# Attention plus GELU layer: softmax reciprocals on GpSimd as a power, with another table that deals score tiles to engines

## Chip, cores and metric

One Trainium2 chip, one core of it. The metric is the device time of one execution in microseconds (us). The kernel before the change takes 746.38 us (median of 3 runs, 745.35 to 746.84).

## Reference

A layer norm of `x` (2048 rows of 512) feeds two branches, and the result is `x` plus both: attention with 32 query heads of 16 columns that share one key and one value head, and a two-layer network of width 1792 with a tanh GELU.

```python
xn = layernorm(x)                                  # (x - mean) / sqrt(var + 1e-5)
q = (xn @ wq) as 32 heads of 16;  k = xn @ wk;  v = xn @ wv
p = softmax(q k^T * 16**-0.5)                      # 2048 x 2048 for each head
a = concat(p v) @ wo
h = gelu(xn @ w1 + b1) @ w2 + b2
out = x + a + h
```

## The kernel before

**Tiling.** The 2048 queries are four blocks of 512. In each block the 32 heads are eight groups of four, so there are 32 passes over a group. In one pass, 16 key tiles of 128 times four heads give 64 score tiles of 128 keys by 512 queries; 2048 such tiles in all. Three consecutive tiles are a unit (683 units), which takes three banks of PSUM; two sets of three banks alternate. TensorE writes the scores of unit u+2 into the banks that unit u has left (`scores`, line 1042).

**Two engines take the exponential.** ScalarE does most tiles with its Exp (`exp`, line 1065), one instruction for the unit's ScalarE tiles, written to buffer `E`. The other tiles go to VectorE: `p1` (line 1096) reads the scores from PSUM and writes 16-bit whole numbers whose bits are a bf16 approximation of the exponential, into buffer `Dt`. `close_batch` then makes three shifted copies of a batch of such tiles (line 1143: one instruction for one copy, one for two copies at once), and subtracts in place once more (line 1139, one tile each, mostly on GpSimd). Each of the five versions is multiplied with a scaled copy of V and summed by TensorE into the bank `pO` (`pv_mm`, line 1109), so that a VectorE tile costs five matmuls and a ScalarE tile one.

**The table.** `DTAB` has one letter for each unit and says which of its three tiles go to VectorE: `.` none, `0` or `o` the first, `2` or `t` the last, `a` or `A` the first two, `b` or `B` the last two, `x` or `X` all. The letters `o t A B X` also end a batch; a batch ends at six tiles at the latest, and at the end of a pass.

**GELU.** After units 182 and 512 ScalarE leaves the exponentials (`GU`) and does four GELU instructions with a table load before and after; around these units the table has `x` and `X`, so that VectorE goes on alone.

**Normalisation.** Column 16 of each head's block of `pO` is the softmax denominator. When a pass ends, `o_evac` copies `pO` to `Of` (line 1155), and DMAs on SyncE's queue take the denominators to `den` (spread over 128 partitions, 16 numbers in each for a pass) and the numerators to `OfP`. After every second pass a reciprocal over `den` (line 1167, both passes together: 128 by 32) runs on VectorE. A DMA takes it to a small DRAM array, eight DMAs bring it back as rows in `rbP`, and GpSimd multiplies `OfP` by `rbP` (line 1186) into `oTp`, which the output projection reads much later. `den`, `OfP` and `rbP` have two buffers that alternate by pairs of passes. The very last pass has its own code (`o_norm_last`, line 1200), which the change leaves alone.

**The order of the work** comes from a planner in the program: every operation is entered with an assumed duration (`occ`), a latency (`lat`) and a due time; `schedule` plays this through once, and each engine then runs its list in that fixed order, with semaphores. GpSimd operations of kind `"pl"` (lines 1139 and 1186) are placed behind the start of a VectorE instruction that is not marked `lock`; VectorE instructions marked `lock` (lines 1143, 1224 and others, SBUF to SBUF in a fast mode) are placed when the plan has GpSimd done. A `"pl"` operation that finds no such place is given to VectorE. Operations entered with `add("pool", ...)` or `setup` without this kind are placed on GpSimd when they are ready, with no regard to VectorE. `PRO_DUE` is a list with one due time for each of the first 338 operations, by position; the last nine of them are the late set-up (`wol`, `selL`, four `wol` DMAs, `wop`, `b2row` and its DMA), and the position after them is the first score operation.

Of the kernel before, what the change touches and what calls it, by code (L numbers as in the profile page):

```python
# [7 lines left out]
ALU = mybir.AluOpType  # L8
AX = mybir.AxisListType

P = 128
# [26 lines left out]
PL_LAT = 0.06  # L38
# [20 lines left out]
DMASK = {".": (), "0": (0,), "2": (2,), "a": (0, 1), "b": (1, 2), "x": (0, 1, 2),  # L59
         "o": (0,), "t": (2,), "A": (0, 1), "B": (1, 2), "X": (0, 1, 2)}  # L60
CLOSE = "otABX"
DTAB = "000to.2t0000t...t0t0..ooo0.o202t2.t..22t2.2t00.t2.0ot2.22o0002..0.o0o.2t22o2o0.00o.o.t.0o2tt.2.2t2o.2o2.20t0.00t22t.222o.2.2o.02.t2o0o.20ooot2.t0o0.t.o0.0t22t.ot.02oo2.2o.t022t0.2000oxXXXot...ooo2tt.202o0t0.t22t.0t2t.22t2ot.2.0oot2o.000.t0ot.20t.to0t02t0o.ot20oo0.20t2o0o..0o.o20o202.0t2t.2.t00oo..2oo020tt.020.t0o0.2.to.222t20o..t000t.2o.ttt22.2too.t.02ot20.t2.o0t0t2o.o0.t002020o..tt220o0.o2o.2t.22tt.o0.02t0oto0.00t.to2t.2.2tt0002t00o.t00.2t22..2o.00otot..2tt2t.t202..o.00t0.o.02o0.ot0t.2t00.tt2t220.0o00o22.2txXxtottot2o.t00t.2tt.ot22oo.tt.ot0.ooot002.to2o.t22o02.oo0o.2oo2t.220oo000.oo02.t.002o002o20.2t22o2t..2o.tttt0tt.2o.00t0t.0o0200t.t22tt00.2tt0.0o20t.0ttot0.2.ot2t..0o.0.."
YF = 664
Y_ALLOW = 2.0
H_ALLOW = 1.0
# [50 lines left out]
class Prog:  # L116
# [19 lines left out]
    def add(self, eng, fn, r=(), w=(), acc=None, dma=None, occ=0.1, lat=0.15, allow=1.0, kind=None, tag=None, after=(), due=None, lock=False, docc=0.0):  # L136
        if len(self.ops) < len(PRO_DUE):
            due = PRO_DUE[len(self.ops)]
        op = _Op()
        op.lock, op.docc = lock, docc  # L140
        op.eng, op.fn = eng, fn
        op.stream = dma or eng
        op.amt = 16 if dma else 1
        op.need = bool(dma)
        op.ticket = None
        op.occ, op.lat, op.allow, op.kind, op.tag = occ, lat, allow, kind, tag
        op.idx = len(self.ops)
        op.done = False
        op.due = due
        op.rel = None  # L150
        op.pm = any(k == ("bank", 7) or k[0] == ("bank", 7) for k in w)
        deps, sdeps = {}, {}

        def dep(o, raw):
            if o is None or o is op:
                return
            if o.stream == eng == "pe":
                sdeps.setdefault(id(o), (o, False))
                return
            deps[id(o)] = o  # L160
            sdeps[id(o)] = (o, True)

        for k in r:
            dep(self.writer.get(k), True)
            for o in self.accs.get(k, ()):
                dep(o, True)
        for k in w:
            dep(self.writer.get(k), False)
            for o in self.readers.get(k, ()):
                dep(o, False)  # L170
            for o in self.accs.get(k, ()):
                dep(o, False)
        if acc is not None:
            dep(self.writer.get(acc), False)
            for o in self.readers.get(acc, ()):
                dep(o, False)
        op.deps = list(deps.values())
        for o in op.deps:
            o.need = True
        for k in w:  # L180
            self.writer[k] = op
            self.readers[k] = []
            self.accs[k] = []
        for k in r:
            self.readers.setdefault(k, []).append(op)
        if acc is not None:
            self.accs.setdefault(acc, []).append(op)
        for o in after:
            sdeps.setdefault(id(o), (o, True))
        if self.in_chain:  # L190
            o = self.chain.get(eng)
            if o is not None:
                sdeps.setdefault(id(o), (o, False))
            self.chain[eng] = op
        op.sdeps = list(sdeps.values())
        self.ops.append(op)
        return op
# [380 lines left out]
def bass_parallel_sum__grouped_kv_mqa__dense_activation_gelu__prompt_kernel(  # L578
# [30 lines left out]
    bf, f32 = dt.bfloat16, dt.float32  # L609
    i16, i32 = dt.int16, dt.int32  # L610

    with ExitStack() as es:
        def sb(shape, dtype, name):
            return es.enter_context(nc.sbuf_tensor(name, shape, dtype))
# [19 lines left out]
        b1T = sb([P, FT], f32, "b1T")  # L634
        ident = sb([P, P], bf, "ident")
        zeros = sb([P, P], bf, "zeros")
        ones = sb([P, P], bf, "ones")
        mask4 = sb([P, 4], bf, "mask4")
        krow = sb([P, 1], i32, "krow")
# [34 lines left out]
        den = sb([P, 2, 2, 16], f32, "den")  # L674
# [14 lines left out]
        add = pr.add  # L689
# [6 lines left out]
        def dve(fn, r=(), w=(), n=TBW, mode=1, allow=1.0, **kw):  # L696
            return add("dve", fn, r, w, occ=vcost(n, mode), lat=dlat[0], allow=allow, **kw)
# [36 lines left out]
        for a, b, t in X_D:  # L734
            nd += 1
            if a is None:
                o, src, w = ((wvk[:, :, Dh:2 * Dh], A_wk, ["wk_s"]), (wvk[:, :, 0:Dh], A_wv, ["wv_s"]))[b]
                src = src.rearrange("(k p) n -> p k n", p=P)
            else:
                o, src, w = x_sb[:, a:b, :], (x_view[:, a // 2, :, :] if b - a == 2 else x_view[:, a // 2, a % 2:a % 2 + 1, :]), [("x", ti) for ti in range(a, b)]  # L740
# [6 lines left out]
        def setup(fn, r=(), w=(), occ=0.16, due=0.0, lat=0.1, **kw):  # L747
            return add("pool", fn, r, w, occ=occ, lat=lat, due=due, **kw)
# [19 lines left out]
              w=[(k, g, j) for k in ("QT", "QTm") for g in range(NGR) for j in range(HG)])  # L768
        setup(lambda e: e.tensor_copy(wkp[:, :, :, 0:Dh], wvk[:, :, Dh:2 * Dh].unsqueeze(2).to_broadcast([P, DT, 4, Dh])),
              r=["wk_s", "wkp"], w=["wkp"], occ=0.35, due=2.0)  # L770
# [8 lines left out]
              r=["mrow"], w=["isc"], due=10.0)  # L779
# [10 lines left out]
        for gl in range(2):  # L790
            setup(lambda e, gl=gl: e.tensor_copy(sel_diag[gl], mask8[:, 4 * gl:4 * gl + 4].unsqueeze(1).to_broadcast([P, NGR // 2, HG])),
                  r=["mask8", "sel8"], w=["sel8"], due=12.0)
# [3 lines left out]
                    n=1500, due=0.01)  # L796
# [177 lines left out]
        for ft, bk in H_PRO:  # L974
# [4 lines left out]
            due=0.0)  # L979
# [3 lines left out]
            r=["khm", "kcm"], w=[B(3), "kb", "krow"], n=40, due=0.0)  # L983
# [5 lines left out]
        for va, vb_ in ((0, NVA), (NVA, NT)):  # L989
# [3 lines left out]
               w=[vbank(va, vb_)[1], ("Vf", va)], due=DU["vf"])  # L993
            r = ["V1", ("Vf", va)]
            ad(lambda e, va=va, vb_=vb_: e.activation(V1[:, 0, va:vb_, 0:Dh], Vf[:, va:vb_, :], ACT.Copy),
               lambda e, va=va, vb_=vb_: e.tensor_copy(V1[:, 0, va:vb_, 0:Dh], Vf[:, va:vb_, :]), (vb_ - va) * Dh, (vb_ - va) * Dh,
               w=[("V", 0, va)], ra=r, rd=r, mode=2, due=DU["vf"] + 0.1)
# [7 lines left out]
                setup(f, occ=0.93, due=20.0, **rw)  # L1005

        late = [pr.writer["krow"]]
        setup(lambda e: e.memset(wol[:], 0.0), w=["wol"], occ=0.4, due=24.0, after=late)
        setup(lambda e: e.tensor_copy(selL[:], ident[:, 16:113:32]), r=["ident"], w=["selL"], due=24.0, after=late)
        dma("sp", wop[:], A_wo.rearrange("(g p) n -> p g n", p=P), "d_wo", w=["wop"], after=late)  # L1010
# [142 lines left out]
        def o_evac(gg):  # L1153
            i = gg % 2
            dve(lambda e: e.tensor_copy(Of[:, i, :], pO), w=["O", ("Of", i)], allow=0.0)  # L1155
            row = Of[16:17, i, :]
            pp, h = divmod(gg, 2)
            s, sl = pp % 2, pp % NPR
            end = gg == NTB * NGR - 2
            dma("sp", den[:, s, h, :], bass.AP(row.tensor, row.offset, [[32 * row.ap[0][0], HG], [1, TBW]]),  # L1160
                f"d_den{i}", r=[("Of", i)], w=[("den", s, h)])
            for j in range(HG):
                r0 = 64 * h + Dh * j
                dma("sp", OfP[r0:r0 + Dh, s, :], Of[32 * j:32 * j + Dh, i, :], f"d_of{s}{h}", r=[("Of", i)], w=[("OfP", s, h, j)])
            if h or end:
                hs = range(h + 1)
                dve(lambda e: e.reciprocal(den[:, s, 0:h + 1, :], den[:, s, 0:h + 1, :]), r=[("den", s, hh) for hh in hs],
                    w=[("den", s, hh) for hh in hs], n=120 + 16 * h)
                dma("sp", rd_dram[gg - h:gg + 1, :].rearrange("g (p c) -> p g c", p=P), den[:, s, 0:h + 1, :], f"d_rd{s}",
                    r=[("den", s, hh) for hh in hs], w=[("rd", s)])  # L1170
                for hh in hs:
                    for j in range(HG):
                        r0 = 64 * hh + Dh * j
                        src = rd_dram[gg - h + hh:gg - h + hh + 1, j * TBW:(j + 1) * TBW]
                        dma("sp", rbP[r0:r0 + Dh, s, :], bass.AP(src.tensor, src.offset, [[0, Dh], [1, TBW]]), f"d_rb{s}",
                            r=[("rd", s)], w=[("rbP", s, hh, j)])
            if end:
                dve(lambda e: e.memset(oTp[64:P, sl, :], 0.0), r=[("Of", i)], w=[("oTp", sl)], n=200, lock=True)
            if h or end:
                n = 64 if end else P  # L1180
                keys = [(k, s, hh, j) for k in ("OfP", "rbP") for hh in range(h + 1) for j in range(HG)]
                first = pre.pop(sl, [])
                for q in range(2):
                    c = slice(q * TBW // 2, (q + 1) * TBW // 2)
                    onorm[gg - h] = onorm[gg] = add(
                        "pool", lambda e, c=c: e.tensor_tensor(oTp[0:n, sl, c], OfP[0:n, s, c], rbP[0:n, s, c], ALU.mult),  # L1186
                        keys, [("oTp", sl, q)] + first, occ=ON_OCC, lat=PL_LAT, allow=PL_DUE, kind="pl", lock=True,
                        docc=vcost(TBW // 2))
# [166 lines left out]
        first, n = None, 0  # L1355
# [101 lines left out]
```

## Time and profile before

| what | value |
|---|---|
| median of 3 runs | 746.38 us |
| the profiled execution | 746.57 us |
| its span, first to last instruction | 744.8 us |
| what lies around the span in that execution | 1.77 us |
| score tiles to ScalarE / to VectorE (from the table) | 1493 / 555 |

The busy time of an engine is the union of its instructions' records; consecutive records of ScalarE and of VectorE overlap, so that a busy share of 100% doesn't mean that the engine could take no more. Rows of the view by line give the line, the engine, the operation, output and inputs, count, busy time, the mean of one in ns, and the idle time before. Windows are stretches of the span with each engine's busy time.

### The profile page before, as it was taken

Reading aid. Unit: us, or ns where it says so; the run is one execution under the profiler, and the core shown is the slowest. Engines: PE = TensorE matmul, PEld = TensorE weight load, DVE = VectorE, ACT = ScalarE, POOL = GpSimd, SP = SyncE. Lnnn points to the kernel's source line nnn. Section 1 sums busy time; section 2 is a strip of 40 time slices with the busy share of each in tenths; the row PEclk is TensorE's granted clock in tenths of the full one; section 3 lists DMA queues with packets and bytes.
Section 4 is the critical chain, followed back from the end, with each engine's and each line's share of the span. In section 5 each row is a group of like instructions: output and inputs, shape, how many; then the busy total and the mean of one; then the engine's idle time right before and its main releaser. Section 6 shows DMA issues by size and latency. Waiting matters only on the chain.

```text
span 744.8 us, 22099 instructions
## 1 busy us (share of the span) xinstructions
PE 730.0 (98%) x9040; PEld 215.0 (29%) x9042; DVE 731.1 (98%) x1412; ACT 729.7 (98%) x741; POOL 383.1 (51%) x548
## 2 busy tenths in 40 slices
PE   7999999999999999999999999999998999999998
PEld 4322222222232222222222222222232222222223
DVE  7999999999999999999999999999999999999996
ACT  8899999999999999999999999999999999999995
POOL 7434555545533546545656455343543646546560
PEclk9999999999999999999999999999999999999999
DMA  9200100000011010100101110100100101010011
GB/s 310 66 19 17 30 11 19 22 11 16 16 46 30 13 35 18 24 16 16 32 7 26 26 38 18 37 16 15 24 12 24 31 17 38 16 46 17 10 31 37
DMA packets 31198, 23.34 MB, mean 31 GB/s; under 512 B 16385, under 2 KB 25722, under 8 KB 31098
## 3 DMA queue, kind: packets, MB, share of 16 engines
q1 hardware_dynamic: 31098, 21.94, 11.2%
q8 instruction: 72, 1.18, 0.7%
q14 instruction: 28, 0.23, 0.1%
HBM read 13.08 MB, written 2.35 MB: 21 GB/s over the span
## 4 chain that ended last, share of the span: by engine, by line
ACT 62%; PE 22%; DVE 13%; DMA 1%; SPq 1%; issue 1%
ACT E L1065 62%; PE pAll L1109 10%; PE pAll L1042 6%; DVE Dt L1096 6%; PE pAll L714 5%; DVE Dt L1143 5%; DMA b1row<-in_B_b_dram 1%; SPq L721 1%; DVE Of L1155 1%; PE pAll L708 0%; PE pAll L1418 0%; DVE Dt L1139 0%; DVE x_sb L1251 0%; DVE xnT L864 0%; DVE qp L1223 0%
## 5 line engine op out<-in xcount | busy, mean ns | idle before, releaser
L1065 ACT ACTIVATE E<-pAll 128x1024 bf16<-128x1024 f32 (+1 forms) x676 | 680.5, 1285 | 1.6 <-PE pAll L1042 1.5
L1139 POOL TENSOR_SCALAR Dt<-Dt 128x512 int16<-128x512 int16 x454 | 342.3, 754 | 325.9 <-DVE Dt L1143 116.0
L1109 PE MATMUL pAll<-Dt,V 128*32 128x512 bf16 x2775 | 409.4, 386 | 2.6 <-DVE Of L1155 2.3
L1096 DVE TENSOR_SCALAR Dt<-pAll 128x512 int16<-128x512 f32 (+1 forms) x541 | 367.6, 693 | 1.9 <-PE pAll L1042 1.0
L1109 PE MATMUL pAll<-E,V 128*32 128x512 bf16 x1493 | 303.9, 384 | 0.2 <-DVE Of L1155 0.2
L1143 DVE TENSOR_SCALAR Dt<-Dt 128x1024 int16<-128x1024 int16 (+6 forms) x540 | 288.0, 559 | 0.4
L1042 PE MATMUL pAll<-QT,KT 32*128 32x512 bf16 x2048 | 267.4, 385 | 4.5 <-ACT E L1065 2.4
L1042 PEld LDWEIGHTS pAll<-QT,KT 32*128 32x128 bf16 x2048 | 66.8, 91 | 295.3 <-ACT E L1065 283.8
L1109 PEld LDWEIGHTS pAll<-Dt,V 128*32 128x32 bf16 x2775 | 103.3, 95 | 102.5 <-issue 69.6
L1109 PEld LDWEIGHTS pAll<-E,V 128*32 128x32 bf16 x1493 | 72.9, 95 | 44.0 <-issue 33.0
L714 PE MATMUL pAll<-xnT,w_sb 128*32 128x512 bf16 x896 | 84.9, 384 | 0.0
L714 PE MATMUL pAll<-w_sb,x_sb 128*32 128x512 bf16 x448 | 76.4, 384 | 0.0
L714 PE MATMUL pAll<-w_sb,ub 128*32 128x512 bf16 x448 | 64.3, 383 | 0.1
L714 PE MATMUL pAll<-wop,oTp 128*32 128x512 bf16 x256 | 51.9, 383 | 0.0
L1186 POOL TENSOR_TENSOR oTp<-OfP,rbP 128x256 bf16<-128x256 f32 (+1 forms) x28 | 22.5, 809 | 14.6 <-DVE Dt L1143 7.9
L714 PEld LDWEIGHTS pAll<-xnT,w_sb 128*32 128x32 bf16 x896 | 21.4, 95 | 26.6 <-issue 16.8
L714 PE MATMUL pAll<-xnT,wq_sb 128*32 128x512 bf16 x256 | 26.8, 383 | 0.0
L1139 DVE TENSOR_SCALAR Dt<-Dt 128x512 int16<-128x512 int16 x101 | 26.2, 279 | 0.0
L1155 DVE COPY Of<-pAll 128x512 f32<-128x512 f32 x31 | 21.1, 680 | 0.1
L714 PEld LDWEIGHTS pAll<-w_sb,x_sb 128*32 128x32 bf16 x448 | 18.3, 95 | 8.2 <-issue 6.7
L1251 DVE TENSOR_SCALAR ub<-pAll,b1T 128x512 bf16<-128x512 f32 x28 | 20.7, 738 | 0.0
L1251 DVE TENSOR_SCALAR x_sb<-pAll,b1T 128x512 bf16<-128x512 f32 x28 | 20.7, 738 | 0.0
(125 smaller groups left out, 264.5 us busy)
## 6 DMA issues: line engine op xcount, KB each, us to landing
OfP<-Of SPq DMA_DIRECT2D x124, 32.0 KB, 2.0
rbP<-rden_rows SPq DMA_DIRECT2D x124, 32.0 KB, 1.8
w_sb<-in_B_w_dram SPq DMA_DIRECT2D x2, 1792.0 KB, 11.4
x_sb<-in_A_x_dram SPq DMA_DIRECT2D x18, 128.0 KB, 2.3
QT<-qp SPq DMA_DIRECT2D x124, 16.0 KB, 1.8
x_sb<-in_A_x_dram SPq DMA_DIRECT2D x7, 256.0 KB, 3.9
out_dram<-x_sb SPq DMA_DIRECT2D x12, 128.0 KB, 1.9
wq_sb<-in_A_wq_dram SPq DMA_DIRECT2D x1, 512.0 KB, 5.9
```

Of the source, the lines that this page charges most:

```text
L714: add("pe", lambda e, c=c, j=j: e.matmul(o[c, :], l[:, c], rh, start=start, stop=stop, tile_position=(0, 32 * j)), r, [(k, j) for k in w] ...
L721: return add(eng, lambda e: e.dma_start(o, i), r, w, dma=stream, occ=occ, lat=lat, allow=allow, **kw)
L1042: ins = e.matmul(o, l, rh, start=True, stop=True, tile_position=(q0, 0))
L1065: o = act(lambda e: e.activation(E[:, s0:s0 + na, :], bank(b0, na).rearrange("p (a n) -> p a n", a=na), ACT.Exp, scale=LN2 / 128.0), w=[B( ...
L1096: op = dve(lambda e: e.tensor_scalar(Dt[:, s:s + n, :], bank(bk, n).rearrange("p (a n) -> p a n", a=n), float(127 * 128) + SPL_D, SPL_MIN, ...
L1109: add("pe", lambda e, a, b: e.matmul(pO[32 * j:32 * j + 32, :], V1[:, v, kt, :], rhs, start=a, stop=b, tile_position=(0, 32 * j)), r=r + [ ...
L1139: add("pool", lambda e, d=d, k=k: e.tensor_scalar(d, d, 1.0, float(k), ALU.mult, ALU.add), [], [(("D", base[o > 0] + q), o)], occ=PL_OCC, ...
L1143: dve(lambda e, d=view(o, nb), q=view(i, nb), k=k: e.tensor_scalar(d, q, float(k), None, ALU.add), r=keys(i), w=keys(o), n=nb * n * TBW, m ...
L1155: dve(lambda e: e.tensor_copy(Of[:, i, :], pO), w=["O", ("Of", i)], allow=0.0)
L1186: "pool", lambda e, c=c: e.tensor_tensor(oTp[0:n, sl, c], OfP[0:n, s, c], rbP[0:n, s, c], ALU.mult),
L1251: dve(lambda e: e.tensor_scalar(ubs[tb % 2][:, ft, :], pM, b1T[:, ft:ft + 1], None, ALU.add), r=["b1T"], w=M4 + [ukey(tb, ft)], n=TBW + 57 ...
```

## The change

The reciprocals at line 1167 become an element-wise power on GpSimd: `den` to the power of a constant tile `neg1` that holds -1.0, in f32. The tile is filled once in the late set-up, ahead of `wol`. The operation is entered without the kind `"pl"`, with an assumed duration of 0.6 us. The reciprocals of the last pass stay on VectorE. The table `DTAB` is another one, of the same length.

```diff
-DTAB = "000to.2t0000t...t0t0..ooo0.o202t2.t. ... 2000oxXXXot... ... 22.2txXxtottot ... 2ot2t..0o.0.."
+DTAB = "0202o0.0t20to...0t02..022o..022o2t.t. ... o2oo.xXX.Xtt22 ... 000.2Xx2xoA..oo ... 20tot..00..."
...
+        neg1 = sb([P, 2, 16], f32, "neg1")
...
         late = [pr.writer["krow"]]
+        setup(lambda e: e.memset(neg1[:], -1.0), w=["neg1"], due=24.0, after=late)
         setup(lambda e: e.memset(wol[:], 0.0), w=["wol"], occ=0.4, due=24.0, after=late)
...
-                dve(lambda e: e.reciprocal(den[:, s, 0:h + 1, :], den[:, s, 0:h + 1, :]), r=[("den", s, hh) for hh in hs],
-                    w=[("den", s, hh) for hh in hs], n=120 + 16 * h)
+                add("pool", lambda e: e.tensor_tensor(den[:, s, 0:h + 1, :], den[:, s, 0:h + 1, :], neg1[:, 0:h + 1, :], ALU.pow),
+                    ["neg1"] + [("den", s, hh) for hh in hs], [("den", s, hh) for hh in hs], occ=0.6, lat=PL_LAT, allow=0.0)
```

Of the two tables, the parts shown in the middle are units 178 to 190 and 508 to 521, around the two GELU stretches. What the two tables say, counted by the rules above:

| | before | after |
|---|---|---|
| tiles to VectorE | 555 | 555 |
| Exp instructions of 3, 2, 1 tiles | 141, 535, 0 | 143, 531, 2 |
| `p1` instructions | 541 | 539 |
| batches | 270 | 253 |

More of the change, by code (lines that the diff above doesn't have):

```diff
@@ L61 @@
 CLOSE = "otABX"
-DTAB = "000to.2t0000t...t0t0..ooo0.o202t2.t..22t2.2t00.t2.0ot2.22o0002..0.o0o.2t22o2o0.00o.o.t.0o2tt.2.2t2o.2o2.20t0.00t22t.222o.2.2o.02.t2o0o.20ooot2.t0o0.t.o0.0t22t.ot.02oo2.2o.t022t0.2000oxXXXot...ooo2tt.202o0t0.t22t.0t2t.22t2ot.2.0oot2o.000.t0ot.20t.to0t02t0o.ot20oo0.20t2o0o..0o.o20o202.0t2t.2.t00oo..2oo020tt.020.t0o0.2.to.222t20o..t000t.2o.ttt22.2too.t.02ot20.t2.o0t0t2o.o0.t002020o..tt220o0.o2o.2t.22tt.o0.02t0oto0.00t.to2t.2.2tt0002t00o.t00.2t22..2o.00otot..2tt2t.t202..o.00t0.o.02o0.ot0t.2t00.tt2t220.0o00o22.2txXxtottot2o.t00t.2tt.ot22oo.tt.ot0.ooot002.to2o.t22o02.oo0o.2oo2t.220oo000.oo02.t.002o002o20.2t22o2t..2o.tttt0tt.2o.00t0t.0o0200t.t22tt00.2tt0.0o20t.0ttot0.2.ot2t..0o.0.."
+DTAB = "0202o0.0t20to...0t02..022o..022o2t.t.22to.20.o0t.ot0t.020t.20.0.o2002t0t..t2t02o0.0o.t.2t.o200o00.t2.t2.22t2.t2o220.o222o2.t2o..0t02t..0oo22t2t2.22t..t0t00to.t.ot2t2000.o.20.0t.oo2oo.xXX.Xtt22t2222o.t.0o0tt0t.tt.o2t2t020.000..2oo202t.t.o0t0.t00.t.otoo20o02t.2o.t2t0oot022t0.00.2tt00o..0o0t22o0.02.0.2t002.0.o2t202ot.o.o0.20ooo..0tt2ttt.2ot22.0to.0000.o0t.o00t2t20.2o00o.02.tto.0t.0t02000o2o.00.o.2o20o202..222o2o2.o2o2.2o2.t.2t022o202ot..2o0.o2to.020.o022t2..22o000t..to..002o..002o22.ot.22.0o22o.202t00o2.20000.2Xx2xoA..ooot2o20t2.ott22t.00t0t.22oo02.o002.tt.toB0..o0o0o20t..t00.ot2o2o200o0.2oto.2t.2tot.00oo0.2ot000.2t020t22o0..t2t00o00t..0o00tt02tt2.0ot0.o..2o.o0.t02o20tot..00..."
 YF = 664
```

## Prediction

> **What bounds the kernel now.** The page comes first: the span, the busy times and the shares of the chain of waits.
>
> ```profile
> span 744.8 us, 22099 instructions
> PE 730.0 (98%) x9040; PEld 215.0 (29%) x9042; DVE 731.1 (98%) x1412; ACT 729.7 (98%) x741; POOL 383.1 (51%) x548
> ACT 62%; PE 22%; DVE 13%; DMA 1%; SPq 1%; issue 1%
> ```
>
> Three engines stand at 98%, so a busy share names no bound. The chain runs 62% of its time through ScalarE and 13% through VectorE. Windows show where ScalarE has time left (after the stretch and its length: busy time of PE, its weight loads, VectorE, ScalarE, GpSimd; clock, DMA share, GB/s).
>
> ```profile
> 100.00:200.00 100.00, 99.27 (x1232) 28.09 (x1224) 99.68 (x184) 100.00 (x100) 54.44 (x75) 1.00 0.07 16
> 200.00:300.00 100.00, 99.59 (x1246) 29.43 (x1242) 99.57 (x189) 99.62 (x93) 47.70 (x64) 1.00 0.10 26
> 300.00:400.00 100.00, 99.34 (x1213) 28.53 (x1212) 99.92 (x187) 100.00 (x101) 55.05 (x71) 1.00 0.09 20
> ...
> 500.00:600.00 100.00, 96.96 (x1205) 28.78 (x1202) 99.39 (x188) 98.90 (x91) 50.10 (x71) 0.98 0.10 23
> 600.00:700.00 100.00, 98.96 (x1271) 27.37 (x1267) 99.77 (x197) 100.00 (x103) 54.70 (x70) 1.00 0.09 22
> ...
> 734.00:744.80 10.80, 8.04 (x112) 3.69 (x110) 4.42 (x12) 2.86 (x4) 0.00 (x0) 1.00 0.15 49
> ```
>
> ScalarE is idle for 0.38 us in one of these and 1.10 us in another, the two with the GELU stretches, and never in the rest: 1.48 us in all. The last 10.8 us are a tail in which no engine is full. The view of waits says who holds whom.
>
> ```profile
> PEld pAll L1042 <- ACT E L1065: 283.8, 656, 0.8
> ...
> PEld pAll L1042 <- DVE Dt L1096: 8.0, 18, 0.7
> PEld pAll L1109 <- DVE Of L1155: 5.1, 7, 2.8
> PEld pAll L1109 <- POOL Dt L1139: 4.3, 18, 0.4
> ...
> ACT E L1065 <- PE pAll L1042: 1.5, 3, 1.0
> ```
>
> The score matmuls wait for ScalarE's Exp 656 times and for VectorE's first step (L1096) 18 times. Outside the GELU stretches the loop is Exp, scores into the freed banks, Exp; VectorE's share of a unit is nearly always done by then. A faster VectorE is therefore worth something only where it ends a wait.
>
> **The reciprocals leave VectorE.**
>
> ```profile
> L1167 DVE RECIPROCAL den<-den 128x32 f32<-128x32 f32 x15 | 5.1, 340 | 0.0
> L1167 DVE RECIPROCAL den<-den 128x16 f32<-128x16 f32 x1 | 0.2, 243 | 0.0
> ...
> L1143 DVE TENSOR_SCALAR Dt<-Dt 128x1024 int16<-128x1024 int16 x189 | 76.3, 415 | 0.1
> L1143 DVE TENSOR_SCALAR Dt<-Dt 128x512 int16<-128x512 int16 x110 | 29.5, 280 | 0.0
> ```
>
> Removed: 15 x 0.340 + 0.243 = 5.3 us of records. The records overlap, so the time between starts is what VectorE really gets back:
>
> ```profile
> 207.66 0.68 DVE L1096 TENSOR_SCALAR Dt<-pAll 128x512 int16<-128x512 f32 x1
> 208.26 0.34 DVE L1167 RECIPROCAL den<-den 128x32 f32<-128x32 f32 x1
> 208.52 0.65 DVE L1096 TENSOR_SCALAR Dt<-pAll 128x512 int16<-128x512 f32 x1
> ```
>
> The next instruction starts 0.26 us after the reciprocal: 15 x 0.26 + 0.16 (0.24 less the same 0.08) = 4.1 us.
>
> **The table.** ScalarE keeps 1493 tiles in 676 Exp instructions (before 141 + 535, after 143 + 531 + 2).
>
> ```profile
> L1065 ACT ACTIVATE E<-pAll 128x1024 bf16<-128x1024 f32 x535 | 527.0, 1197 | 1.2 <-PE pAll L1042 1.2
> L1065 ACT ACTIVATE E<-pAll 128x1536 bf16<-128x1536 f32 x141 | 224.0, 1619 | 0.3 <-PE pAll L1042 0.3
> ```
>
> If an Exp costs a fixed part and a part for each tile, as these rows allow (0.42 us more for the third tile), equal tiles in equal instructions cost the same: 0. The one-tile form has no row; for its two instructions I take nothing and bound it by 0.1 us each. TensorE keeps its matmuls: 555 x 5 + 1493. VectorE loses 17 batches, 34 instructions of L1143: their elements stay, and by the two L1143 rows the fixed part is 0.280 - (0.415 - 0.280) = 0.145 us, about 0.07 us less between starts by the overlap above: 34 x 0.07 = 2.4 us, 4.9 us at most by the records. Two fewer instructions of L1096 are 0.2 us. VectorE's relief is thus 4.1 + 2.4 + 0.2 = 6.7 us between starts, about 0.9% of its 731.1 us.
>
> What that buys: at least 0, since ScalarE is full; at most the chain's VectorE share in proportion, 13% of 744.8 = 97 us times 0.9% = 0.9 us. I take 0.6, nearer to the top, because the chain's long VectorE pieces are real and the rest is cover by ScalarE.
>
> **The two GELU stretches.** These rows show ScalarE coming back from its GELU work, and the scores it waits for.
>
> ```profile
> 224.25 0.10 PEld L1042 LDWEIGHTS pAll<-QT,KT 32*128 32x128 bf16 x3 [0.42 <-DVE Dt L1096]
> 226.53 0.39 PE L1042 MATMUL pAll<-QT,KT 32*128 32x512 bf16 x3
> 226.97 2.79 ACT L1065 ACTIVATE E<-pAll 128x1536 bf16<-128x1536 f32 x2 [0.32 <-PE pAll L1042]
> 228.70 0.39 PE L1042 MATMUL pAll<-QT,KT 32*128 32x512 bf16 x3
> ...
> 568.18 1.94 ACT L1065 ACTIVATE E<-pAll 128x1024 bf16<-128x1024 f32 x2
> 571.11 4.85 ACT L1065 ACTIVATE E<-pAll 128x1024 bf16<-128x1024 f32 x5 [0.99 <-PE pAll L1042]
> ```
>
> Before, units 183 to 186 and 513 to 515 are all VectorE's; ScalarE returns at 187 and 516 and then idles 0.32 and 0.99 us: 1.31. After, the runs are 183 to 185 and 513 to 514, with 186 (three ScalarE tiles) and 515 (two) ahead of one more all-VectorE unit each. VectorE has three tiles fewer to do before ScalarE's return, so both old holes should go: -1.3. But behind 186 ScalarE's next work is 188, whose scores need the banks of 186: its Exp (1.62) must end, then a start of the matmuls (226.97 + 1.62 = 228.59 to 228.70, so 0.11), the scores (0.39) and the step to the Exp (226.53 + 0.39 to 226.97, so 0.05). That leaves 0.11 + 0.39 + 0.05 = 0.55 us idle, and as much behind 515: +1.1. Together -0.2 us. Bounds: -1.3 if the plan finds cover, +2 if VectorE is also late there.
>
> **What GpSimd gets.** Sixteen powers. The trace has no power; the nearest rows on GpSimd:
>
> ```profile
> L1139 POOL TENSOR_SCALAR Dt<-Dt 128x512 int16<-128x512 int16 x454 | 342.3, 754 | 325.9 <-DVE Dt L1143 116.0 <-PE pAll L1109 73.4 <-DVE Dt L1096 58.6
> L1186 POOL TENSOR_TENSOR oTp<-OfP,rbP 128x256 bf16<-128x256 f32 x27 | 21.7, 812 | 11.8 <-DVE Dt L1143 5.2 <-DVE Dt L1139 3.2 <-DVE Dt L1096 1.1
> ...
> L767 POOL MEMSET QT<- 128x2048 f32 x1 | 1.8, 1799 | 0.0
> L837 POOL TENSOR_TENSOR nmr<-nm,rstd 128x1 f32<-128x1 f32 x6 | 1.4, 229 | 0.3 <-issue 0.2
> ```
>
> A two-input operation costs 0.229 us for one column and 0.812 for 256, so 32 columns of a plain product would be 0.3. A power is more work per element; the far end is the longest row, 1.8 us. I take 0.8, the row of the same kind with two f32 inputs: 16 x 0.8 = 13 us on an engine that is idle half the time. Behind a power on GpSimd stand L1139s; who waits for these is TensorE, 18 times in 454, 4.3 us, none over 0.4. With 16 powers, half with an L1139 close behind (8 x 4.3/18 = 1.9 us if all of these delayed TensorE), I charge a tenth, +0.2; bounds 0 and 1.9. On SyncE's queue the DMA of the reciprocals waits for the power, with the eight row DMAs and whatever x or query load the plan put next behind it.
>
> ```profile
> POOL Dt L1139 <- DMA rbP<-rden_rows: 2.4, 1, 2.4
> ```
>
> This is the only wait for these transfers that the view shows, one of GpSimd's at the last pair; TensorE, ScalarE and VectorE have none, so half a us on that path costs 0 (if the cover were gone, the half us once, at the last pair). The fill of `neg1` is one more set-up instruction, about 0.2 us as the smallest row above; it shifts the late set-up's due times by one place, which reorders work needed after unit 180: 0 (without that cover, 0.2).
>
> The powers also have no place of their own in VectorE's order.
>
> ```profile
> 140.17 0.62 POOL L1139 TENSOR_SCALAR Dt<-Dt 128x512 int16<-128x512 int16 x1 [1.68 <-DVE Dt L1143]
> 140.60 1.27 DVE L1143 TENSOR_SCALAR Dt<-Dt 128x4096 int16<-128x4096 int16 x1
> ...
> L1143 DVE TENSOR_SCALAR Dt<-Dt 128x4096 int16<-128x4096 int16 x24 | 29.2, 1217 | 0.0
> ```
>
> Here L1143 began 0.19 us before GpSimd's end and took 1.27 us where 1.217 is the mean: only 0.05 us longer. The Trainium skill, "SBUF — State Buffer", section "SBUF: two separate sides", speaks against the change more strongly: VectorE in a two-port mode and GpSimd take the shared ports for a whole instruction, and the other one blocks. By that rule a fast VectorE instruction that meets a fresh 0.8 us power stands for up to 0.8 us, 13 us over sixteen; this row agrees in direction with 0.05 us.
>
> Without the page, from the page of the profile:
>
> ```profile
> L1143 DVE TENSOR_SCALAR Dt<-Dt 128x1024 int16<-128x1024 int16 (+6 forms) x540 | 288.0, 559 | 0.4
> ```
>
> L1143 is 288.0 of VectorE's 731.1 us, 40%, so some six powers may meet one; a meeting costs 0.05 us by the row above and at most the power. VectorE's time spent this way is 0.3 to 5 us; since its work is mostly early, it counts as 0 and bounds at +2.
>
> **The sum**, against the profiled execution's own 746.57 us (span 744.8 and 1.77 around it; 0.19 above the median of 746.38): 746.57 - 0.6 - 0.2 + 0.2 = 746.0. Against the median it is 745.8. I predict **745.9 us**.
>
> **Rivals.** *Faster, 744.0:* the new table closes all visible holes of ScalarE (-1.5) and the relief reaches its top (-0.9). For it: the holes lie where VectorE was heaviest, and that part of the table changed most. Against it: the new order makes its own holes behind 186 and 515.
>
> *Slower, 749:* the power is long, about the 1.8 us of the far row. The plan allows 0.6, so each power leaves GpSimd 1.2 us late; the next L1139s, and the fast VectorE instructions that meet the power, move behind it, L1096 behind those, and the banks come free late. Place: the 16 pair ends, 2 us after each second copy of `pO`. Price: a quarter of 1.2 us reaching ScalarE, 16 x 0.3 = 4.8, less 1.0 for the gains: 750; with 0.2 us reaching it, 749. It decides from about 1.1 us, where the lateness passes the 0.4 us that TensorE waits at most today. Against it: GpSimd's gaps, 326 us before L1139. The Trainium skill's rule on the shared ports, above, would add blocked VectorE instructions to the same price.
>
> *Slower by the table, 748:* the two new holes come on top, as VectorE's postponed copies fall into them (+2). *No effect of the relief:* 746.6, inside the forecast.
>
> **How the numbers follow.** A measurement of this kernel tells 0.2%, 1.5 us, from no change. Forecast and no effect together 0.35; faster rival 0.34; long power 0.21; table 0.10. Their sides: faster 0.34, same 0.35, slower 0.31. The forecast's own range is 744.9 to 747.9. The range for 8 in 10 takes in the faster rival with its bound of -1.3 and the nearer half of the slower ones: 743.3 to 748.9.
>
> **What would show it.** Right: the windows with ScalarE at 100.00 stay so, its idle time in the two GELU windows is about 1 us in all, VectorE's busy time falls by 6 to 10 us, and the power's row reads 0.5 to 1 us. Long power: its row above 1.1 us, the waits of TensorE for GpSimd's L1139 well over 4.3 us, longer L1143s of one form. Wrong altogether: Exp waits spread over all windows, or a changed tail after the last Exp.

## The result, and the profile after

The changed kernel takes 792.42 us (median of 4 runs, 788.69 to 795.12) against 746.26 before: a ratio of 1.0614, with a 95% interval of 1.0591 to 1.0637. The forecast was 745.9. The profiled execution took 788.69 us, 42.1 more than the one of before, and all of that is in the span (787.0 for 744.8, 42.2 more).

The page of the changed kernel: the span, the busy times, the chain by engine.

```profile
span 787.0 us, 22091 instructions
PE 746.0 (95%) x9066; PEld 220.3 (28%) x9066; DVE 742.3 (94%) x1388; ACT 735.9 (94%) x741; POOL 451.1 (57%) x538
PE 47%; DVE 39%; ACT 5%; issue 4%; POOL 3%; DMA 1%; SPq 1%; POOLq 0%
```

All three full engines have become less busy in share, and the chain has left ScalarE: 5% in place of 62%. The windows show where (stretch and length; then the busy time of PE, weight loads, VectorE, ScalarE, GpSimd; at the end the granted clock, the DMA share and GB/s).

```profile
100.00:200.00 100.00, 93.81 (x1128) 25.76 (x1124) 91.50 (x161) 91.72 (x91) 59.70 (x69) 0.97 0.07 15
...
300.00:400.00 100.00, 92.13 (x1041) 26.12 (x1035) 88.32 (x167) 88.09 (x88) 62.98 (x70) 0.95 0.08 19
...
776.00:787.00 11.00, 8.06 (x114) 3.65 (x107) 5.01 (x13) 3.09 (x4) 0.00 (x0) 1.00 0.14 48
```

Before, VectorE and ScalarE were at 99.68 and 100.00 in the first of these windows; now both lose 8 and then 12 us in 100. The tail is as it was: from the end of the last Exp to the end of the span it is 8.9 us in both traces. GpSimd's groups say what is new:

```profile
L1141 POOL TENSOR_SCALAR Dt<-Dt 128x512 int16<-128x512 int16 x427 | 318.2, 745 | 290.5 <-DVE Dt L1145 107.1 <-PE pAll L1111 73.0 <-DVE Dt L1141 30.4
L1169 POOL TENSOR_TENSOR den<-den,neg 128x32 f32<-128x32 f32 x15 | 89.1, 5942 | 7.0 <-DMA den<-Of 5.9
L1169 POOL TENSOR_TENSOR den<-den,neg 128x16 f32<-128x16 f32 x1 | 2.9, 2900 | 0.1
```

A power over 32 columns takes 5.94 us, where the reciprocal on VectorE took 0.340 and the planner assumes 0.6. The waits that grew:

```profile
ACT E L1067 <- PE pAll L1044: 36.3, 31, 5.4
PEld pAll L1111 <- POOL Dt L1141: 34.1, 34, 3.8
DVE Dt L1098 <- PE pAll L1044: 30.6, 21, 5.6
PE pAll L1111 <- POOL Dt L1141: 22.7, 14, 3.5
```

The wait of TensorE's weight loads for GpSimd's subtractions (L1139 before, L1141 now) went from 4.3 us to 34.1; the 22.7 us of the matmuls themselves are in part the same stalls, counted on the other row. ScalarE's wait for scores went from 1.5 to 36.3. One power shows the order of events (timeline: start, duration, engine, line; idle time before it and what ended it):

```profile
79.67 6.24 POOL L1169 TENSOR_TENSOR den<-den,neg 128x32 f32<-128x32 f32 x1
85.99 3.41 POOL L1141 TENSOR_SCALAR Dt<-Dt 128x512 int16<-128x512 int16 x5
...
87.36 0.09 PEld L1111 LDWEIGHTS pAll<-Dt,V 128*32 128x32 bf16 x1 [3.50 <-POOL Dt L1141]
...
77.16 8.36 ACT L1067 ACTIVATE E<-pAll 128x1024 bf16<-128x1024 f32 x8
89.25 2.54 ACT L1067 ACTIVATE E<-pAll 128x1024 bf16<-128x1024 f32 x2 [3.73 <-PE pAll L1044]
...
84.77 0.68 DVE L1145 TENSOR_SCALAR Dt<-Dt 128x2048 int16<-128x2048 int16 x1
89.25 0.69 DVE L1098 TENSOR_SCALAR Dt<-pAll 128x512 int16<-128x512 f32 x1 [3.81 <-PE pAll L1044]
```

Five subtractions stand behind the power and then run back to back. TensorE, in its fixed order, stands for 3.50 us in front of a matmul on one of these tiles, with the next scores behind it; ScalarE and VectorE then have no scores for 3.7 and 3.8 us.

TensorE does not come back at full speed either. Here are windows of 2 us around the end of this stall, and two score matmuls:

```profile
86.00:88.00 2.00, 0.64 (x12) 0.32 (x13) 0.00 (x0) 0.00 (x0) 1.84 (x3) 1.00 0.08 8
88.00:90.00 2.00, 2.00 (x15) 0.32 (x10) 0.74 (x2) 0.74 (x1) 1.24 (x3) 0.50 0.42 63
90.00:92.00 2.00, 2.00 (x20) 0.51 (x21) 1.10 (x2) 1.74 (x3) 1.53 (x1) 0.65 0.28 56
...
88.60 0.61 PE L1044 MATMUL pAll<-QT,KT 32*128 32x512 bf16 x3
91.55 0.39 PE L1044 MATMUL pAll<-QT,KT 32*128 32x512 bf16 x3
```

The granted clock is 0.50 and 0.65 of full speed there, and the scores take 0.61 us in place of 0.39. The trace has seven such stretches at half clock before the end of the work, 27 us together, each within 2 us of the end of a stall of TensorE of 2.0 to 3.5 us; the trace of before has one, of 3.4 us. The mean clock fell from 0.998 to 0.983. If TensorE had set the time throughout, that would be 0.015 x 787 = 12 us, which is an estimate from above: part of the loss follows from the stalls in this way, and no run separates it.

### The profile page after: what moved, and what is told of

Read it like the earlier page. It is cut to its first block, busy times and chain, and to the rows that moved or that the text cites. A ratio compares the mean times of both kernels' runs of the same rounds, so it can differ in the third digit from the quotient of the medians.

```text
span 787.0 us, 22091 instructions
## 1 busy us (share of the span) xinstructions
PE 746.0 (95%) x9066; PEld 220.3 (28%) x9066; DVE 742.3 (94%) x1388; ACT 735.9 (94%) x741; POOL 451.1 (57%) x538
## 3 DMA queue, kind: packets, MB, share of 16 engines
HBM read 13.08 MB, written 2.35 MB: 20 GB/s over the span
## 4 chain that ended last, share of the span: by engine, by line
PE 47%; DVE 39%; ACT 5%; issue 4%; POOL 3%; DMA 1%; SPq 1%; POOLq 0%
PE pAll L1111 21%; DVE Dt L1098 18%; PE pAll L1044 15%; DVE Dt L1145 14%; PE pAll L715 10%; ACT E L1067 5%; POOL Dt L1141 2%; DVE Dt L1141 2%; POOL den L1169 1%; DMA b1row<-in_B_b_dram 1%; DVE Of L1157 1%; PE pAll L1420 1%; DVE ub L1253 1%; SPq L722 1%; DVE x_sb L1253 1%
## 5 line engine op out<-in xcount | busy, mean ns | idle before, releaser
L1067 ACT ACTIVATE E<-pAll 128x1024 bf16<-128x1024 f32 (+1 forms) x676 | 686.7, 1196 | 37.4 <-PE pAll L1044 36.3
L1141 POOL TENSOR_SCALAR Dt<-Dt 128x512 int16<-128x512 int16 x427 | 318.2, 745 | 290.5 <-DVE Dt L1145 107.1
L1111 PE MATMUL pAll<-Dt,V 128*32 128x512 bf16 x2775 | 412.6, 390 | 26.2 <-POOL Dt L1141 22.7
L1098 DVE TENSOR_SCALAR Dt<-pAll 128x512 int16<-128x512 f32 x540 | 367.4, 697 | 31.0 <-PE pAll L1044 30.6
L1145 DVE TENSOR_SCALAR Dt<-Dt 128x1024 int16<-128x1024 int16 (+6 forms) x506 | 296.1, 609 | 1.0 <-PE pAll L1111 0.6
L1111 PE MATMUL pAll<-E,V 128*32 128x512 bf16 x1493 | 295.6, 388 | 0.8 <-DVE Of L1157 0.7
L1169 POOL TENSOR_TENSOR den<-den,neg 128x32 f32<-128x32 f32 (+1 forms) x16 | 92.0, 5752 | 7.2 <-DMA den<-Of 5.9
L715 PE MATMUL pAll<-xnT,w_sb 128*32 128x512 bf16 x896 | 89.1, 389 | 0.1
L715 PE MATMUL pAll<-w_sb,x_sb 128*32 128x512 bf16 x448 | 72.3, 384 | 0.0
L715 PE MATMUL pAll<-w_sb,ub 128*32 128x512 bf16 x448 | 68.5, 393 | 0.0
L1141 DVE TENSOR_SCALAR Dt<-Dt 128x512 int16<-128x512 int16 x128 | 34.3, 295 | 0.0
L715 PE MATMUL pAll<-xnT,wq_sb 128*32 128x512 bf16 x256 | 22.7, 383 | 0.0
```

The costliest lines, as they stand in the source:

```text
L715: add("pe", lambda e, c=c, j=j: e.matmul(o[c, :], l[:, c], rh, start=start, stop=stop, tile_position=(0, 32 * j)), r, [(k, j) for k in w] ...
L1067: o = act(lambda e: e.activation(E[:, s0:s0 + na, :], bank(b0, na).rearrange("p (a n) -> p a n", a=na), ACT.Exp, scale=LN2 / 128.0), w=[B( ...
L1098: op = dve(lambda e: e.tensor_scalar(Dt[:, s:s + n, :], bank(bk, n).rearrange("p (a n) -> p a n", a=n), float(127 * 128) + SPL_D, SPL_MIN, ...
L1111: add("pe", lambda e, a, b: e.matmul(pO[32 * j:32 * j + 32, :], V1[:, v, kt, :], rhs, start=a, stop=b, tile_position=(0, 32 * j)), r=r + [ ...
L1141: add("pool", lambda e, d=d, k=k: e.tensor_scalar(d, d, 1.0, float(k), ALU.mult, ALU.add), [], [(("D", base[o > 0] + q), o)], occ=PL_OCC, ...
L1145: dve(lambda e, d=view(o, nb), q=view(i, nb), k=k: e.tensor_scalar(d, q, float(k), None, ALU.add), r=keys(i), w=keys(o), n=nb * n * TBW, m ...
```

## The experiments

The theory after the result is the queue: the power is 5 us longer than the order knows, the subtractions behind it on GpSimd come late, and TensorE carries that to the others. Its rivals: the new order itself, the SBUF ports that GpSimd shares with VectorE, and the transfers on SyncE's queue that wait for the reciprocals. Undoing a part in the source makes the planner write another order. So the first five runs keep the changed kernel's planned order of every engine and change what one operation does.

**A product in the power's place.**

```diff
-... neg1[:, 0:h + 1, :], ALU.pow)
+... neg1[:, 0:h + 1, :], ALU.mult)
```

> The same planned order on every engine as in the changed kernel; only the operation is a product of the denominators with the constant tile, so the reciprocals are left out and the attention part of the output is wrong. Queue theory (the power takes 5.9 us where the plan has 0.6, and what stands behind it on GpSimd is late): the product takes about 0.3 us, nothing is late, time 745 to 750 us, and ScalarE's idle time before the Exp falls from 37 us to under 5. Order theory (the new table and the place of the operation in the order cost the time, whatever its length): above 765 us.

748.52 us, 1.0028 of before (1.0019 to 1.0038). From the page and the views by line and of waits:

```profile
PE 730.2 (98%) x9064; PEld 217.0 (29%) x9066; DVE 732.1 (98%) x1388; ACT 730.0 (98%) x741; POOL 370.5 (50%) x538
L1169 POOL TENSOR_TENSOR den<-den,neg 128x32 f32<-128x32 f32 x15 | 8.7, 582 | 7.0 <-DMA den<-Of 5.9
L1141 DVE TENSOR_SCALAR Dt<-Dt 128x512 int16<-128x512 int16 x128 | 32.8, 282 | 0.0
PEld pAll L1111 <- POOL Dt L1141: 4.3, 16, 0.7
ACT E L1067 <- PE pAll L1044: 2.7, 5, 1.6
```

The waits are back at 4.3 and 2.7 us. About 44 of the 46 us go with one operation, 16 times, being a power; the rest of the change, the new order with its table, costs 2.3 us. Two things in these rows bear on the prediction. VectorE's busy time is 732.1 us, not below the 731.1 of before: it does 128 subtractions in place of 101. And the hole for want of the banks of unit 515 is longer than forecast, 1.58 us in this timeline, against 0.26 for those of unit 186 (in both places the new order has one other Exp in between):

```profile
227.39 12.90 ACT L1067 ACTIVATE E<-pAll 128x1024 bf16<-128x1024 f32 x13 [0.26 <-PE pAll L1044]
...
572.09 3.71 ACT L1067 ACTIVATE E<-pAll 128x1024 bf16<-128x1024 f32 x3 [1.58 <-PE pAll L1044]
```

**Shorter powers.** Half of the columns, and a quarter:

```diff
-... e.tensor_tensor(den[:, s, 0:h + 1, :], den[:, s, 0:h + 1, :], neg1[:, 0:h + 1, :], ALU.pow)
+... e.tensor_tensor(den[:, s, 0:h + 1, 0:8], den[:, s, 0:h + 1, 0:8], neg1[:, 0:h + 1, 0:8], ALU.pow)
```

> Same planned order; the power covers 8 of the 16 columns of each pass, the rest of the denominators are not inverted. The power should take about 2.9 us. Queue theory with slack: of the changed kernel's 5.1 us of lateness for each power some 2.6 us reached the end (42 us over 16), so about 2.5 us were absorbed; 2.3 us of lateness is then mostly absorbed: 747 to 756 us. If every late us costs the same (no slack): 42 x 2.3 / 5.1 = 19 us, about 766 us. Order theory: above 780 us, as the changed kernel.

> Same planned order as the changed kernel; the power covers 4 of the 16 columns of each pass, the rest of the denominators are not inverted. From 2.90 us for 16 columns and 5.43 for 32 without a wait inside, about 1.6 us. Queue theory with slack: between the product (748.5) and the half power (759.7), and below the straight line between them, so 748 to 752 us. If each us of lateness costs the same: the half power is 2.8 us longer than the product and costs 11.2, so 1.3 us more than the product would give 754 us.

759.72 us (1.0179, 1.0160 to 1.0198) and 752.85 us (1.0090, 1.0075 to 1.0105). The operation's rows, half and then quarter:

```profile
L1169 POOL TENSOR_TENSOR den<-den,neg 128x16 f32<-128x16 f32 x15 | 50.8, 3386 | 7.0 <-DMA den<-Of 5.9
```

```profile
L1169 POOL TENSOR_TENSOR den<-den,neg 128x8 f32<-128x8 f32 x15 | 33.6, 2243 | 7.0 <-DMA den<-Of 5.9
```

| mean length, us | time, us | more for each us of length | mean granted clock |
|---|---|---|---|
| 0.58 (product) | 748.52 | | 0.998 |
| 2.24 | 752.85 | 2.6 | 0.997 |
| 3.39 | 759.72 | 6.0 | 0.995 |
| 5.94 | 789.41 (next run) | 11.6 | 0.978 |

Time against length bends upward. At the steep end 16 powers cost 11.6 us for each us, 0.7 us of every late one. It looks like slack of a us or two in the order, and the clock, which falls along with the time, adds to it; how much of the bend is either was not tried. Neither expectation was met: the half power lies above the 747 to 756 of a queue with slack and below the 766 of a straight line, the quarter just above the 748 to 752 and below the 754. The quarter's mean length was 2.24 us where 1.6 was expected.

**The power without anyone waiting for it.** It writes a scratch tile, and the DMA of the denominators waits for their landing alone; the waits were exchanged after the planning.

```diff
-        pr.schedule()
+        pr.schedule()
+        for rdo, po in unhook:
+            rdo.deps = [o for o in rdo.deps if o is not po] + po.deps
```

> Same planned order and the full power of 5.9 us in its place on GpSimd, but it writes a scratch tile and no one waits for it: the DMA of the reciprocals takes the denominators as they came, so the reciprocals are left out. Queue theory (what is late is GpSimd's own subtractions, line 1141): 785 to 800 us, as the changed kernel. Chain theory (SyncE's queue stands for the power, and the rows and query heads behind it come late): 746 to 755 us.

789.41 us (1.0582, 1.0558 to 1.0607; the changed kernel's interval overlaps it, its median is 3.0 us higher), with TensorE's waits for the subtractions where they were:

```profile
PEld pAll L1113 <- POOL Dt L1143: 34.1, 34, 3.8
PE pAll L1113 <- POOL Dt L1143: 22.8, 14, 3.5
```

The transfers behind the reciprocals play little or no part, some 3 us by the medians. What is left is the power's place on GpSimd, ahead of the subtractions.

**As long as the half power, but moving data.**

```diff
-... e.tensor_tensor(den[...], den[...], neg1[...], ALU.pow)
+... e.tensor_tensor(pad[:, 0:h + 1, :], w1_sb[:, 0:h + 1, 0:592], w1_sb[:, 2:h + 3, 0:592], ALU.mult)
```

> Same planned order; in the place of the power a product of two bf16 pieces of the weights, 128 by 1184, into a scratch tile, so that GpSimd reads and writes SBUF all through; the reciprocals are left out. By the row of the 256-column product it should take 2.5 to 3 us, as long as the half power in the run beside it. If only the length matters (queue): the same time as that run within 3 us. If GpSimd's data traffic holds VectorE's fast instructions for the whole of it (the Trainium skill, SBUF - State Buffer, section SBUF: two separate sides): fast instructions of line 1145 that fall into it last up to 3 us longer, and the time is 10 to 30 us above that run.

779.28 us (1.0445, 1.0418 to 1.0472), 20 us above the half power although the operation is shorter, 2.84 us. Its row, and one of them, GpSimd and then VectorE (timeline of this run):

```profile
L1170 POOL TENSOR_TENSOR pad<-w_sb 128x1184 bf16<-128x1184 bf16 x15 | 42.6, 2839 | 7.0 <-DMA den<-Of 5.9
...
166.13 2.44 POOL L1170 TENSOR_TENSOR pad<-w_sb 128x1184 bf16<-128x1184 bf16 x1
...
166.50 2.35 DVE L1146 TENSOR_SCALAR Dt<-Dt 128x1024 int16<-128x1024 int16 x1
```

And one power of the changed kernel:

```profile
173.55 5.43 POOL L1169 TENSOR_TENSOR den<-den,neg 128x32 f32<-128x32 f32 x1
...
173.93 0.42 DVE L1145 TENSOR_SCALAR Dt<-Dt 128x1024 int16<-128x1024 int16 x1
174.26 0.68 DVE L1098 TENSOR_SCALAR Dt<-pAll 128x512 int16<-128x512 f32 x1
174.86 0.28 DVE L1145 TENSOR_SCALAR Dt<-Dt 128x512 int16<-128x512 int16 x1
...
175.66 0.69 DVE L1145 TENSOR_SCALAR Dt<-Dt 128x2048 int16<-128x2048 int16 x1
```

The same fast instruction takes 2.35 us under the product and 0.42 inside the power, which is what it takes alone. The product blocks VectorE until it is done; the power, twice as long, does not. This holds for all of them: 89 fast instructions (L1145, L1141) lie across one of the 16 powers, and all together they are 0.9 us longer than usual; under the long products 30 are 25 us longer. So what the power itself does to the ports is no cause of the changed kernel's loss.

What stands behind the power is another matter. The late subtractions run back to back on GpSimd, and fast instructions that meet them get longer. A power of the changed kernel with its queue, an instruction beside it that usually takes 0.68 us, and one form's row with the product and with the power:

```profile
277.03 6.10 POOL L1169 TENSOR_TENSOR den<-den,neg 128x32 f32<-128x32 f32 x1
283.21 4.86 POOL L1141 TENSOR_SCALAR Dt<-Dt 128x512 int16<-128x512 int16 x6
...
287.52 1.10 DVE L1145 TENSOR_SCALAR Dt<-Dt 128x2048 int16<-128x2048 int16 x1
...
L1145 DVE TENSOR_SCALAR Dt<-Dt 128x512 int16<-128x512 int16 x85 | 23.4, 280 | 0.0
...
L1145 DVE TENSOR_SCALAR Dt<-Dt 128x512 int16<-128x512 int16 x85 | 25.4, 305 | 0.0
```

In the whole trace of the changed kernel the same fast instructions have 11 us more of records than with the product. Of the 33 outside the powers that are over 0.1 us longer than usual, 30 begin less than 10 us behind one. These 11 us are a share of the loss that comes by way of the queue; what they do to the end was not separated.

**The planner told.** Now the order may change: the power's assumed duration is set to what it takes. Then the same with another table, from some thousands of steps of a search against the planner.

```diff
-... occ=0.6, lat=PL_LAT, allow=0.0)
+... occ=3.0 * (h + 1), lat=PL_LAT, allow=0.0)
```

> The full power, correct reciprocals, the new table; only the planner's assumed duration is 6.0 us for two passes instead of 0.6, so that the order knows of it. If the loss is a surprise to a fixed order (lateness theory), TensorE's waits for line 1141 fall from 57 us to under 12 and the time is set by the new order instead. If GpSimd's lost 92 us is a loss in itself, whatever the order, no order gets it back: the time stays within 15 us of 789. The new table was made for another order, so a loss of 15 to 35 us against 746 is expected from that alone: 760 to 785.

> As the run with the planner told, with a table that some thousands of steps of a search against the planner gave for this program (250 letters differ from the changed kernel's). If a good order can hide the power, 746 to 755 us. If GpSimd's time is a real loss (its subtractions go to VectorE, which has no room), above 758 us; I expect 760 to 770.

774.27 us (1.0375, 1.0360 to 1.0391) and 763.49 us (1.0235, 1.0217 to 1.0252), both with all reciprocals computed. From the second:

```profile
PE 742.5 (98%) x9066; PEld 224.3 (29%) x9066; DVE 746.0 (98%) x1504; ACT 734.2 (96%) x741; POOL 390.7 (51%) x462
L1141 DVE TENSOR_SCALAR Dt<-Dt 128x512 int16<-128x512 int16 x199 | 51.1, 282 | 0.0
PEld pAll L1111 <- POOL Dt L1141: 4.0, 14, 0.7
```

TensorE's surprise waits are gone (4.0 us, and 4.5 in the first), as the theory has it, and the price has moved: 199 subtractions are on VectorE in place of 101 before, and its busy time rises by 15 us over before. Together the two get back 29 of 46 us, 18 by telling the planner. That no order could hide the power isn't shown; this search found none.

**The table alone**, on the kernel before, with the reciprocals on VectorE:

```diff
-DTAB = "000to.2t0000t... ..."
+DTAB = "0202o0.0t20to... ..."
```

> The kernel before with nothing but the new table; reciprocals on VectorE. If the table is good or bad by itself (its batches, its places around the GELU), 743 to 750 us, as the run with the product in the power's place. If a table fits only the exact program that it was made for, because the planner's greedy order falls apart otherwise: above 760 us, with correct reciprocals on VectorE and no long operation on GpSimd anywhere.

769.04 us (1.0315, 1.0296 to 1.0333). Its view of waits and by line:

```profile
ACT E L1065 <- PE pAll L1109: 17.5, 7, 5.1
L1139 DVE TENSOR_SCALAR Dt<-Dt 128x512 int16<-128x512 int16 x172 | 44.3, 280 | 1.9 <-PE pAll L1109 1.8
```

The same table is in the product run, where it and all the rest of the change cost 2.3 us, and costs 23 us in the order that the planner makes here; here 172 subtractions went to VectorE. Read as "undo one part", this run would put half of the loss on the table, and the product run shows that to be false.

**What VectorE's relief is worth.** The kernel before in its own order, with each reciprocal done twice:

```diff
+                    e.reciprocal(pw[:, 0:h + 1, k, :], den[:, s, 0:h + 1, :])
                     return e.reciprocal(den[:, s, 0:h + 1, :], den[:, s, 0:h + 1, :])
```

> The kernel before, in its own planned order, with every reciprocal of the main part done twice on VectorE (the first one into a scratch tile): VectorE gets 15 x 0.26 + 0.16 = 4.1 us more, as much as the change took from it. If VectorE's time is on the path that sets the end: +4 us, about 750.2. If the reciprocals lie beside ScalarE's Exp, whose idle time outside the GELU stretches is nil: 746 to 747 us, a difference of at most 0.6 us.

746.79 against 746.65 us, a ratio of 1.0004 (0.9995 to 1.0014). The second reciprocal of each pair:

```profile
L1171 DVE RECIPROCAL den<-den 128x32 f32<-128x32 f32 x15 | 4.4, 292 | 0.0
```

These 4.4 us reach the end with 0.14 us, which is nothing within the interval; it allows 1 us at most. So 4 us more on VectorE cost little or nothing in this order, and 4 us less can hardly have had more to give. That is an argument from adding; the removal alone was not run.

## Why the prediction was wrong

*The bound.* "A faster VectorE is worth something only where it ends a wait" holds as far as the doubled reciprocal shows, which cost nothing that could be measured. The 0.6 us put down for the relief lies within that run's interval and is not to be told from 0.

*What GpSimd gets.* This is the step that failed. The power was taken at 0.8 us, "the row of the same kind with two f32 inputs", with 1.8, the longest row on GpSimd, as far end. It measured 5.94, where the product of the same data took 0.58. A row of another operation says what the data of a power cost to move; it is no bound from above on what is computed for each element. The range inherited that end: its slower side, up to 748.9, was priced with 1.8 us.

*The charge for the queue.* The chain was named (L1139s behind the power, TensorE behind these), but charged at 0.2 us from the waits of before. Those describe an order that knew its durations. With a lateness of 5.3 us over the assumed 0.6, the run with no one waiting for the power's result lies 41 us above the product (789.4 - 748.5): this is the price of the queue, with the lower clock behind the stalls and the longer VectorE instructions beside the late subtractions in it.

*The slower rival* had the place and most of the mechanism, 16 pair ends and a late GpSimd. Its threshold of about 1.1 us fits the runs (2.24 us costs 4.3 us more than the product), though none lies between 0.58 and 2.24. It was priced for 1.8 us and given a fifth of the chances. Its fast VectorE instructions that stand behind the power did not come about, and the clock was not in it.

*The ports.* Counted 0 with a bound of +2 from one meeting that cost 0.05 us. For the power 0 is right, but not for the reason given there: a product of half the length does block VectorE for its whole time. The Trainium skill, "SBUF — State Buffer", section "SBUF: two separate sides", has an instruction of either engine hold the shared pair to its end; the product's 2.35 us agrees, and the power's row (a fast instruction of 0.42 us in its midst) does not. What the term left out is the late subtractions, behind which fast instructions were 11 us longer in all in the changed kernel.

*The table.* The sum had +1.1 for the holes behind units 186 and 515, and they measured 0.26 + 1.58 = 1.84 us, 0.5 more than the 1.31 of before where the sum had 0.2 less. VectorE's 6.7 us of relief left out that another order can put more subtractions on VectorE: 27 more, 27 x 0.282 = 7.6 us of records, took it all. Whether the powers or the table put them there isn't shown; in the run of the table alone, with no power, there are 172. With a short operation the change is 2.3 us slower than before, where the sum had 0.6 faster.

*The fill of the constant and the shifted due times* were costed at nothing; the product run, which has both, leaves at most its 2.3 us for them and the table together. They weren't tried apart.

## What to carry to other kernels

An operation that no row shows has no upper bound in rows of other operations: where it enters an in-order queue ahead of work that a full engine waits for, price it by what each us of lateness costs, and let the range reach to where that breaks the kernel. An order planned in advance pays for a wrong duration on every engine behind it: here about half of each late us came through to the end (41 us for 16 powers that were 5.3 us late), less of a short delay and more of a long one. To undo one part of a change in such a kernel, hold the planned order fixed and change what the one instruction does; a table or a switch put back alone tests another order.

## What the runs showed of the hardware

A GpSimd power in f32 took 2.90 us for 128 by 16 and 5.43 for 128 by 32 at best, so about 0.16 us for each column and 0.4 fixed; 1.64 at best for 128 by 8 fits that; VectorE's reciprocal of the larger shape took 0.340. VectorE's fast SBUF instructions kept their usual durations inside the powers (89 of them, 0.9 us longer in all), but under a GpSimd product of 2.44 us one of them took 2.35 in place of 0.42. Behind a stall of TensorE of 3.2 us the granted clock was 0.50 for 3.4 us, and the matmul records lasted 0.61 us in place of 0.39. A second reciprocal straight behind the first took 0.292 us in place of 0.340.
